# FFN output with h stationary, weights and v by casting DMA, filler matmuls: a sketch attention and ReGLU FFN on one core

## Chip, cores, metric

One core of a Trainium2 chip. The metric is the device time of one execution in microseconds (us), as the median of several. A measurement of this kernel tells about 1% from no change.

## What is computed

Polynomial-sketch attention, then a ReGLU FFN on its output:

```python
# q, k, v: (4, 4, 1088, 32); S1, S2: (8, 32); w_gate, w_val: (128, 1536); w_out: (1536, 128)
def phi(x):                                   # (..., 32) -> (..., 64)
    a = einsum('rd,bhsd->bhsr', S1, x); b = einsum('rd,bhsd->bhsr', S2, x)
    return einsum('bhsi,bhsj->bhsij', a, b).reshape(*x.shape[:-1], 64)
q_p, k_p = phi(q), phi(k)
kv  = einsum('bhsf,bhsd->bhfd', k_p, v)
z   = sum(k_p, axis=2)
num = einsum('bhsf,bhfd->bhsd', q_p, kv)
den = einsum('bhsf,bhf->bhs', q_p, z)[..., None] + 1e-6
x   = (num / den).transpose(0, 2, 1, 3).reshape(4352, 128)
out = (maximum(x @ w_gate, 0) * (x @ w_val)) @ w_out
```

## The kernel before

The 4352 tokens are cut into eight FFN chunks of 512 (two of each batch) and a ninth of 256 with the rest of all batches (`REST`). An FFN chunk has 12 slots, one for each 128 of d_ff; 108 slots in all, which the code counts as `n`. In a slot PE multiplies xT by a 128x128 piece of w_gate (`ffn_g`, L540) and of w_val (`ffn_v`, L551), ScalarE takes the relu of the first (`ffn_relu`, L545), VectorE multiplies (`ffn_mul`, L556, into ht), and three slots later (`LAG`) PE adds w_out's part to `ot_ps` (`ffn_out`, L384), with w_out stationary and 512 tokens moving, so that the output comes out feature-major. At a chunk's end ScalarE evicts ot to fp16 (`ffn_fin0`, L390), PE transposes it back in pieces of 128 tokens (`ffn_fin1`, L398), ScalarE evicts that to `o_sb` (`ffn_fin2`, L404), and SyncE's queue stores it.

Each batch needs its attention before its two chunks. For k: two VectorE transposes into kT (L175), 16 small fp32 matmuls with S (`k_ab_mm`, L187), two transposes back (kab, L194), products on VectorE or GpSimd (`k_outer`, kp, L210), nine pairs of matmuls with v into kv_ps (`k_kv`, L228), z (`k_z`, L247), its copy zs (`k_zs`), one more matmul (`k_sz`, L257), w_s (`k_sw`), and kvb (`k_fin`). For q: the same transposes, matmuls with S and with w_s (L187, L299), denominator, products (qp, L210), PE transposes (`q_xpose`, L348), eviction on ScalarE (`q_ev`, qpt, L354), the numerator (`q_num`, L369) and xT on ScalarE (`q_x`, L373).

PSUM: two banks each for g and v, one for ot, one for kv, and a ring of two (`ps_a`) for all else: the S matmuls, z, q's transposes, the numerator, and the output's transposes.

Loads: S1 and S2 on ScalarE's queue; k and q on SyncE's; v on GpSimd's, cast to fp16 on the way, in four pieces a batch (`load_v`, L93). Batch 0's v is issued near the start. w_gate and w_val are loaded as fp32 once the second kT transpose of batch 0 is done, w_out behind k of batch 1, and ScalarE casts each to fp16 (`cast_w`, L422). k and q of batch b+1 are issued behind the second q transpose of batch b.

The order on every engine is written out by a planner: each step has a key (its place), an engine, a cost, what it needs and which PSUM buffers it takes and frees. `run` goes through time and gives each engine the first step by key that can start, with landing times from `LAND`; steps of batches 1 to 3 start at T0 = 19 us of its clock at the earliest. The engines then run that order, each strictly in turn, and wait for one another by semaphores.

Of the kernel before, what the change touches and what calls it, by code (L numbers as in the profile page):

```python
# [16 lines left out]
KLEAD, QLEAD, VLEAD, LAG = 40, 20, 44, 3  # L17
WAIT, T0 = 0.02, 19.0
LAND = {"s": 4.8, "k": (5.0, 12.0, 15.0, 20.0), "q": (7.0, 13.0, 16.0, 21.0), "v": 8.0, "w": (11.0, 13.0, 15.0)}
# [3 lines left out]
def kernel(  # L23
# [66 lines left out]
    def load_v(b, g):  # L90
        x = v[b].rearrange("h (t c) d -> t h (c d)", t=32)
        n = NC + 1 if g < 2 else NC
        nc.gpsimd.dma_start(  # L93
            out=v4[b][32 * g:32 * g + 32, :, 0:n].rearrange("p h c d -> p h (c d)"),
            in_=x[:, :, CB[g] * D:(CB[g] + n) * D],
        )
# [7 lines left out]

    w_in = [big.tile([128, NJ, 128], FP32, name=f"w_in{i}") for i in range(3)]
# [13 lines left out]
    for g in range(4):  # L119
        load_v(0, g)  # L120
# [14 lines left out]
    nc.scalar.activation(out=warm, in_=warm, func=ACTF.Relu)  # L135

# [40 lines left out]
    def k_transpose(b, i):  # L177
        transpose_in(kT[b % 2], k4[b], i)

# [3 lines left out]
    def ab_mm(key, xt, n, c0, lo=0):  # L183

        for rp in range(2):
            for g in range(4):
# [35 lines left out]
    def k_kv(b, c):  # L222
        if c == 0:
            st["kv", b] = ps_k.tile([128, 2, 64], FP32, name="kv_ps")
        ps = st["kv", b]
        np = SL if c == NC else 128
        for p in range(2):
            i = nc.tensor.matmul(ps[:, p].rearrange("p (h d) -> p h d", h=2),  # L228
                                 st["kp", b, c][0:np, p * 128:(p + 1) * 128],
                                 v4[b][0:np, 2 * p:2 * p + 2, c],  # L230
                                 start=(c == 0 and p == 0), stop=(c == NC), skip_group_check=True)
            if c == 0 and p == 0:
                first = i
            elif c == 0 and not MANUAL:
                tc.add_manual_dep(
                    i.ins, first.ins.name,
                    mybir.DependencyInfo(mybir.DependencyClass.NoSync, mybir.DependencyReason.DATA),
                    reason="the first one clears the bank's written bits")
# [17 lines left out]
    def k_sz(b):  # L256
        nc.tensor.matmul(st["z", b][:, HR:2 * HR], s1f4.rearrange("p h d -> p (h d)"), st["zs", b],  # L257
                         start=True, stop=True, skip_group_check=True)
# [75 lines left out]
    def q_outer(key, c0, c1, eng):  # L334
        np, m = q_np(key), c1 - c0
        qp = php.tile([128, m, H * F], FP16, name=f"qp{m}")
        outer(eng, qp[0:np].rearrange("p c (h i j) -> p (c h) i j", h=H, i=R),
              st["a2", key][0:np, c0 * H:c1 * H], q_ab(key, 1, c0, c1), np, m * H)
        for c in range(c0, c1):
            st["qp", key, c] = qp[:, c - c0]  # L340


    def q_xpose(key, p0, c):
# [3 lines left out]
        for p in range(2):  # L347
            nc.tensor.transpose(st["qpt", key, p0][:, p, c * n:(c + 1) * n],  # L348
                                st["qp", key, p0 + c][0:n, p * 128:(p + 1) * 128], ident16[0:n, 0:n])

    def q_ev(key, p0):
        n = q_np(key)
        t = php.tile([128, 2, 512], FP16, name="qpt")
        nc.scalar.copy(out=t[:, :, 0:4 * n], in_=st["qpt", key, p0][:, :, 0:4 * n])  # L354
        st["qpts", key, p0] = t

    def q_num(key, p0):
# [4 lines left out]
        if key == REST:  # L362
            for b in range(B):
                for p in range(2):
                    nc.tensor.matmul(ps[64 * p:64 * p + 64, b * n:(b + 1) * n], kvb[b][:, p],
                                     t[:, p, b * n:(b + 1) * n], start=True, stop=True)
            return
        for p in range(2):
            nc.tensor.matmul(ps[64 * p:64 * p + 64], kvb[key[0]][:, p], t[:, p], start=True, stop=True)  # L369
# [9 lines left out]
    def ffn_out(n):  # L379
        i, j = divmod(n, NJ)  # L380
        cs = CH[i][1]
        if j == 0:
            st["ot", i] = ps_o.tile([128, 512], FP32, name="ot_ps")
        nc.tensor.matmul(st["ot", i][:, :cs], wo_sb[:, j], st["ht", i][:, j, :cs],  # L384
                         start=(j == 0), stop=(j == NJ - 1))

    def ffn_fin0(i):
        cs = CH[i][1]
        ot = fo.tile([128, 512], FP16, name="ot16")
        nc.scalar.copy(out=ot[:, :cs], in_=st["ot", i][:, :cs])  # L390
        st["ot16", i] = ot

    def ffn_fin1(i):
        cs = CH[i][1]
        ps = ps_a.tile([128, 4, DM], FP16, name="ps_a")
        st["ott", i] = ps
        for t in range(cs // 128):
            nc.tensor.transpose(ps[:, t], st["ot16", i][:, t * 128:(t + 1) * 128], ident16)  # L398

    def ffn_fin2(i):  # L400
        cs = CH[i][1]
        n = cs // 128
        o = fo.tile([128, 4, DM], FP32, name="o_sb")
        nc.scalar.mul(out=o[:, :n], in_=st["ott", i][:, :n], mul=1.0 / (XSCALE * XSCALE))  # L404
        if n == 4:
# [15 lines left out]
    def cast_w(i):  # L421
        nc.scalar.copy(out=(wg_sb, wv_sb, wo_sb)[i], in_=w_in[i])  # L422

# [6 lines left out]
    RING = {"g": 2, "v": 2, "o": 1, "k": 1, "a": 2}  # L430
    LAT = {"PE": 0.24, "ACT": 0.16, "DVE": 0.15, "POOL": 0.2, "SP": 0.0}
# [4 lines left out]
    def run():  # L436
# [5 lines left out]
        while any(todo.values()):  # L442
            best = None
            for e, q in todo.items():
                pick = None
                for s in q:
                    if any(n not in made for n in s[6]):
                        continue
                    t = max([clock[e], s[10]] + [made[n] for n in s[6]])
# [18 lines left out]
            todo[s[2]].remove(s)  # L468
            for r in s[8]:
# [10 lines left out]
    def plan_k(b, s, pieces, d=1.0, t0=0.0):  # L480
# [11 lines left out]
        at(s + 6 * d, "PE", 0.45, k_z, b, need=[("kab", b)], make=("z", b), take="a")  # L492
        at(s + 8 * d, "DVE", 0.12, k_zs, b, need=[("z", b)], make=("zs", b))
        at(s + 9 * d, "PE", 0.15, k_sz, b, need=[("zs", b)], make=("sz", b))
        at(s + 11 * d, "DVE", 0.13, k_sw, b, need=[("sz", b)], make=("w", b), free="a")
        for c in range(NC + 1):
            at(s + (8 + 0.8 * c) * d, "PE", 0.075, k_kv, b, c,
               need=[("kp", b, of[c]), ("v4", b), ("kv", b, c - 1) if c else ("kab", b)], make=("kv", b, c),
               take="k" if c == 0 else "")
        at(s + 16 * d, "DVE", 0.22, k_fin, b, need=[("kv", b, NC)], make=("kvb", b), free="k")  # L500
# [62 lines left out]
    made["s"], made["v4", 0] = LAND["s"], LAND["v"]  # L563
    for i in range(3):
        made["win", i] = LAND["w"][i]

    def plan_v(b, s, t0):
        for g in range(4):
            at(s + 0.1 * g, "POOL", 0.65, load_v, b, g, make=("v4i", b, g), t0=t0)
        at(s + 0.5, "SP", 0.01, lambda: None, need=[("v4i", b, g) for g in range(4)], make=("v4i", b))  # L570
        at(s + 0.5, "SP", 2.5, lambda: None, need=[("v4i", b)], make=("v4", b))


    for i in range(3):
        at(-39 + i, "ACT", 1.4, cast_w, i, need=[("win", i)], make=("w", i))
# [15 lines left out]
    for n in range(NSLOT):  # L591
# [58 lines left out]
```

## Time and profile before

| what | value |
|---|---|
| median of 3 runs | 136.62 us (136.24 to 137.31) |
| the profiled execution | 137.69 us, its span 135.6 us |
| busy: PE, VectorE, ScalarE, GpSimd | 104.1, 95.6, 84.6, 50.7 us |
| instructions on PE: matmuls, weight loads | 838, 838 |
| granted clock over the span | 0.969 |

PE is TensorE's matmuls, PEld its loads of the stationary operand, DVE VectorE, ACT ScalarE, POOL GpSimd, SP SyncE; a q behind the name is the engine's queue of DMA issues and control instructions. A matmul's duration in the trace includes its way through the array, so that matmuls in a row overlap: how fast they follow one another is seen in the chain that ended last, where each stands with the time until the next. The granted clock is shown as 1.00 until a change is recorded.

### The profile page before, as it was taken

How to read it: one execution, taken by the hardware profiler on the slowest of the kernel's cores; microseconds unless marked ns; L12 is line 12 of the kernel's file. 1: busy time of each engine (PE TensorE's matmuls, PEld its weight loads, DVE VectorE, ACT ScalarE, POOL GpSimd, SP SyncE). 2: the span in 40 equal slices, each digit the busy share in tenths (PEclk: the TensorE clock that was granted, in tenths of full speed). 3: DMA queues.
4: the chain of work that ended last, by engine and by line, in shares of the span. 5: the costliest groups of instructions: out<-in, count | busy, mean ns of one | idle time of the engine just before them, and what ended most of it. 6: DMA issues, size and time to landing. Idle time of an engine off the chain costs nothing.

```text
span 135.6 us, 2420 instructions
## 1 busy us (share of the span) xinstructions
PE 104.1 (77%) x838; PEld 48.4 (36%) x838; DVE 95.6 (70%) x198; ACT 84.6 (62%) x149; POOL 50.7 (37%) x72
## 2 busy tenths in 40 slices
PE   0007774599999875999779999999999999999100
PEld 0002432224443442334245445445443444465000
DVE  2046888228999774999968769999758999998000
ACT  3000442677266775857838955997999999986200
POOL 7401725937859991001599203946000000000000
PEclk9999999999999999999999999999999999999755
DMA  4935996292635019100011010011011011010110
GB/s 127 220 73 145 357 302 224 28 99 78 252 47 60 0 21 333 43 35 0 6 37 41 6 46 30 2 30 48 0 34 46 7 39 36 25 49 15 47 40 18
DMA packets 7059, 10.33 MB, mean 76 GB/s; under 512 B 776, under 2 KB 4616, under 8 KB 7048
## 3 DMA queue, kind: packets, MB, share of 16 engines
q1 hardware_dynamic: 4324, 8.98, 20.0%
q0 software_dynamic: 2304, 1.12, 7.2%
q10 hardware_dynamic: 420, 0.10, 0.3%
q8 instruction: 6, 0.10, 0.3%
q14 instruction: 5, 0.04, 0.1%
HBM read 9.08 MB, written 2.23 MB: 83 GB/s over the span
## 4 chain that ended last, share of the span: by engine, by line
PE 58%; DMA 14%; DVE 11%; ACT 8%; issue 2%; ACTq 1%; SPq 0%; DVEq 0%
PE v_ps L551 15%; PE g_ps L540 15%; PE ot_ps L384 14%; DVE ht L556 6%; DMA w_in<-in_moe_w_out_dram 6%; DMA xall<-in_S_dram 5%; PE ps_a L187 5%; ACT g_sb L545 4%; DMA k<-in_k_dram 3%; PE ps_a L369 2%; PE ps_a L348 2%; DVE qT L175 1%; PE kv_ps L228 1%; PE ps_a L299 1%; PE ps_a L398 1%
## 5 line engine op out<-in xcount | busy, mean ns | idle before, releaser
L556 DVE TENSOR_TENSOR ht<-g_sb,v_ps 128x512 f16<-128x512 f16 (+1 forms) x108 | 66.5, 649 | 10.2 <-PE v_ps L551 3.3
L545 ACT ACTIVATE g_sb<-g_ps 128x512 f16<-128x512 f32 (+1 forms) x108 | 60.1, 583 | 21.2 <-PE g_ps L540 8.8
L551 PE MATMUL v_ps<-xT,wv_sb 128*128 128x512 f16 (+1 forms) x108 | 40.4, 374 | 1.6 <-DVE ht L556 1.4
L540 PE MATMUL g_ps<-xT,wg_sb 128*128 128x512 f16 (+1 forms) x108 | 39.1, 378 | 2.8 <-ACT g_sb L545 2.3
L384 PE MATMUL ot_ps<-ht,wo_sb 128*128 128x512 f16 (+1 forms) x108 | 39.6, 368 | 0.4
L210 POOL TENSOR_TENSOR kp<-kab 128x512 f16<-128x512 f32 (+2 forms) x16 | 17.0, 1086 | 11.0 <-DVE kab L194 11.0
L210 POOL TENSOR_TENSOR qp<-a,qab 128x512 f16<-128x512 f32 (+2 forms) x18 | 17.6, 1000 | 4.8 <-DVE a L330 3.5
L551 PEld LDWEIGHTS <-wv_sb 128*128 128x128 f16 x108 | 10.6, 98 | 12.8 <-issue 6.7
L384 PEld LDWEIGHTS <-wo_sb 128*128 128x128 f16 x108 | 10.6, 98 | 9.7 <-issue 3.3
L540 PEld LDWEIGHTS <-wg_sb 128*128 128x128 f16 x108 | 10.5, 101 | 10.0 <-issue 2.3
L187 PE MATMUL ps_a<-kT,s_bd 64*32 64x288 f32 x64 | 4.7, 549 | 10.1 <-DVE kT L175 10.1
L348 PE MATMUL ps_a<-ident,qp 128*128 128x128 f16 (+1 forms) x72 | 9.9, 236 | 2.7 <-POOL qp L210 1.5
L315 POOL TENSOR_TENSOR bw<-qab,qw 128x256 f32<-128x256 f32 (+2 forms) x5 | 3.3, 655 | 21.1 <-DVE qw L306 21.1
L348 PEld LDWEIGHTS <-qp 128*128 128x128 f16 (+1 forms) x72 | 6.0, 103 | 10.5 <-POOL qp L210 2.8
L228 PEld LDWEIGHTS <-kp 128*128 128x128 f16 (+1 forms) x72 | 6.0, 105 | 9.6 <-issue 4.2
L93 POOL DMA_DIRECT2D v<-in_v_dram x16 | 9.0, 568 | 0.1
L354 ACT COPY qpt<-ps_a 128x1024 f16<-128x1024 f16 (+1 forms) x9 | 9.0, 999 | 0.0
L228 PE MATMUL kv_ps<-v,kp 128*128 128x64 f16 (+1 forms) x72 | 8.0, 205 | 0.9 <-DVE kp L210 0.9
L422 ACT CAST wg_sb<-w_in 128x1536 f16<-128x1536 f32 x1 | 1.5, 1472 | 11.5 <-DMA w_in<-in_moe_w_gate_dram 11.5
L175 DVE STREAM_TRANSPOSE kT<-k 128x544 f32<-128x544 f32 x8 | 5.5, 718 | 2.8 <-DMA k<-in_k_dram 2.8
L175 DVE STREAM_TRANSPOSE qT<-q 128x544 f32<-128x544 f32 x8 | 5.8, 724 | 2.3 <-DMA q<-in_q_dram 2.3
L373 ACT CAST xT<-ps_a 128x512 f16<-128x512 f32 (+1 forms) x9 | 5.3, 588 | 1.1 <-PE ps_a L369 0.7
(60 smaller groups left out, 71.9 us busy)
## 6 DMA issues: line engine op xcount, KB each, us to landing
q<-in_q_dram SPq DMA_DIRECT2D x4, 544.0 KB
out_dram<-o_sb SPq DMA_DIRECT2D x16, 128.0 KB
k<-in_k_dram SPq DMA_DIRECT2D x3, 544.0 KB
w_in<-in_moe_w_gate_dram SPq DMA_DIRECT2D x1, 768.0 KB
w_in<-in_moe_w_val_dram SPq DMA_DIRECT2D x1, 768.0 KB
w_in<-in_moe_w_out_dram SPq DMA_DIRECT2D x1, 768.0 KB
v<-in_v_dram POOLq DMA_DIRECT2D x8, 72.0 KB, 2.8
k<-in_k_dram SPq DMA_DIRECT2D x2, 272.0 KB
```

Source lines behind the costliest of these rows:

```text
L93: nc.gpsimd.dma_start(out=v4[b][32 * g:32 * g + 32, :, 0:n].rearrange("p h c d -> p h (c d)"), in_=x[:, :, CB[g] * D:(CB[g] + n) * D],)
L175: st["last"] = nc.vector.transpose(out=dst[:, a:e], in_=src[:, a:e])
L187: nc.tensor.matmul(st["ps", key][rp][32 * g:32 * g + 32, lo:lo + 32 * n], s_bd[64 * rp:64 * rp + 64].rearrange("p h r x -> p (h r x)"), xt ...
L210: eng.tensor_tensor(out=dst, in0=a[:, :, :, None].to_broadcast([np, n, R, R]), in1=bb[:, :, None, :].to_broadcast([np, n, R, R]), op=ALU.mult)
L228: i = nc.tensor.matmul(ps[:, p].rearrange("p (h d) -> p h d", h=2), st["kp", b, c][0:np, p * 128:(p + 1) * 128], v4[b][0:np, 2 * p:2 * p + ...
L348: nc.tensor.transpose(st["qpt", key, p0][:, p, c * n:(c + 1) * n], st["qp", key, p0 + c][0:n, p * 128:(p + 1) * 128], ident16[0:n, 0:n])
L354: nc.scalar.copy(out=t[:, :, 0:4 * n], in_=st["qpt", key, p0][:, :, 0:4 * n])
L384: nc.tensor.matmul(st["ot", i][:, :cs], wo_sb[:, j], st["ht", i][:, j, :cs], start=(j == 0), stop=(j == NJ - 1))
L540: nc.tensor.matmul(st["g", n][:, :cs], wg_sb[:, j], xT[:, c0:c0 + cs], start=True, stop=True)
L545: nc.scalar.activation(out=st["gs", n][:, :cs], in_=st["g", n][:, :cs], func=ACTF.Relu)
L551: nc.tensor.matmul(st["v", n][:, :cs], wv_sb[:, j], xT[:, c0:c0 + cs], start=True, stop=True)
L556: nc.vector.tensor_tensor(out=st["ht", i][:, j, :cs], in0=st["gs", n][:, :cs], in1=st["v", n][:, :cs], op=ALU.mult)
```

## The change

- `ffn_out`: h is the stationary operand, in pieces of 128 tokens, and w_out's piece (128 columns) moves; so ot is token-major. The eviction to fp16, the transposes and the second eviction fall away; one eviction (`ffn_fin`) with the scaling writes `o_sb`, and the stores are a step of their own.
- Weights: loaded by GpSimd's queue straight into the fp16 tiles (a cast on the way), behind batch 0's v; no fp32 copies and no casts on ScalarE.
- Batch 0's v is issued behind the first kT transpose of batch 0. S2 goes to GpSimd's queue, ahead of everything else there; S1 stays.
- z lives in kv's bank: `k_z` takes that bank, and its first matmuls clear it; kv and the w_s matmul start without clearing. A bank of the ring of two is not taken any more.
- Filler matmuls (128x128 zeros by 128 columns) fill PE's planned gaps from 2.5 us of the planner's clock until the first g; they use ot's bank.
- The S matmuls go through their column groups in the outer loop; q's products lie in one tile of four; the planner knows the four g_sb buffers.

```diff
-LAND = {"s": 4.8, "k": (5.0, 12.0, 15.0, 20.0), "q": (7.0, 13.0, 16.0, 21.0), "v": 8.0, "w": (11.0, 13.0, 15.0)}
+LAND = {"s": 3.5, "k": (5.2, 12.0, 15.0, 20.0), "q": (6.8, 13.0, 16.0, 21.0)}
+NFILL = 200
...
     def load_v(b, g):
...
+        behind(st["kt0"] if b == 0 else None, i)
...
-    for i, sm in enumerate((S1, S2)):
-        nc.scalar.dma_start(out=xall[:, i], in_=sm[None].to_broadcast([16, R, D]))
+    for sm, i, eng in ((S1, 0, nc.scalar), (S2, 1, nc.gpsimd)):
+        eng.dma_start(out=xall[:, i], in_=sm[None].to_broadcast([16, R, D]))
...
-    def load_w(i, after):
+    def load_w(i):
...
-        behind(after, nc.sync.dma_start(out=w_in[i], in_=x))
+        nc.gpsimd.dma_start(out=(wg_sb, wv_sb, wo_sb)[i], in_=x)
...
+    zeros = const.tile([128, 128], FP16, name="zeros")
+    nc.vector.memset(zeros, 0.0)
...
     def ab_mm(key, xt, n, c0, lo=0):
-        for rp in range(2):
-            for g in range(4):
+        for g in range(4):
+            for rp in range(2):
...
     def k_kv(b, c):
-        if c == 0:
-            st["kv", b] = ps_k.tile([128, 2, 64], FP32, name="kv_ps")
...
-                                 start=(c == 0 and p == 0), stop=(c == NC), skip_group_check=True)
+                                 start=False, stop=(c == NC), skip_group_check=True)
...
     def k_z(b):
-        ps = ps_a.tile([128, 512], FP32, name="ps_a")
-        st["z", b] = ps
+        bank = ps_k.tile([128, 192], FP32, name="kv_ps")
+        st["kv", b] = bank[:, 0:128].rearrange("p (a d) -> p a d", a=2)
+        st["z", b] = ps = bank[:, 128:192]
...
     def ffn_out(n):
         i, j = divmod(n, NJ)
-        cs = CH[i][1]
         if j == 0:
-            st["ot", i] = ps_o.tile([128, 512], FP32, name="ot_ps")
-        nc.tensor.matmul(st["ot", i][:, :cs], wo_sb[:, j], st["ht", i][:, j, :cs],
-                         start=(j == 0), stop=(j == NJ - 1))
-
-    def ffn_fin0(i):
...
-    def ffn_fin1(i):
...
-    def ffn_fin2(i):
...
+            st["ot", i] = ps_o.tile([128, 4, DM], FP32, name="ot_ps")
+        for t in range(CH[i][1] // 128):
+            nc.tensor.matmul(st["ot", i][:, t], st["ht", i][:, j, t * 128:(t + 1) * 128], wo_sb[:, j],
+                             start=(j == 0 and t == 0), stop=(j == NJ - 1), skip_group_check=True)
+
+    def ffn_fin(i):
+        n = CH[i][1] // 128
         o = fo.tile([128, 4, DM], FP32, name="o_sb")
-        nc.scalar.mul(out=o[:, :n], in_=st["ott", i][:, :n], mul=1.0 / (XSCALE * XSCALE))
+        nc.scalar.mul(out=o[:, :n], in_=st["ot", i][:, :n], mul=1.0 / (XSCALE * XSCALE))
+        st["o", i] = o
+
+    def ffn_store(i):
...
-    def cast_w(i):
-        nc.scalar.copy(out=(wg_sb, wv_sb, wo_sb)[i], in_=w_in[i])
...
+            if ("g", 0) in made:
+                todo["PE"] = [s for s in todo["PE"] if s[4] is not fill]
...
+    plan_v(0, -50, 0, need=[("kT", 0, 0)])
     for i in range(3):
...
-        at(-39 + i, "ACT", 1.4, cast_w, i, need=[("win", i)], make=("w", i))
+        at(-49 + i, "POOL", (0.8, 0.6, 1.1)[i], load_w, i, make=("wi", i), t0=0.0, need=[("v4i", 0, 3)])
+        at(-49 + i, "NONE", 5.0, None, need=[("wi", i)], make=("w", i))
...
+    def fill():
+        if "fill" not in st:
+            st["fill"] = ps_o.tile([128, 4, DM], FP32, name="ot_ps")
+        nc.tensor.matmul(st["fill"][:, 0], zeros, zeros, start=True, stop=True)
+
+    for n in range(NFILL):
+        at(1000 + n, "PE", 0.1, fill, t0=2.5)
```

## Rows read from the trace of the kernel before

**Rows 1.** Windows: length, busy us (instructions) by engine, clock, DMA share, GB/s.

```profile
9.00:18.00 9.00, 5.91 (x82) 2.89 (x83) 6.84 (x17) 2.42 (x2) 3.27 (x4) 1.00 0.66 221
...
26.60:52.00 25.40, 23.81 (x208) 10.70 (x208) 18.44 (x38) 16.50 (x29) 19.45 (x23) 1.00 0.46 94
52.00:106.00 54.00, 50.46 (x409) 22.93 (x405) 45.21 (x86) 42.45 (x76) 18.58 (x20) 1.00 0.12 39
106.00:119.00 13.00, 13.00 (x64) 5.96 (x63) 12.61 (x20) 12.49 (x23) 0.00 (x0) 1.00 0.09 28
```

**Rows 2.** The page's chain that ended last: shares of the span by engine.

```profile
PE 58%; DMA 14%; DVE 11%; ACT 8%; issue 2%; ACTq 1%; SPq 0%; DVEq 0%
```

**Rows 3.** The same chain in order of time, 0 to 36 us: start, us, what.

```profile
1.57 7.09 DMA xall<-in_S_dram
...
10.14 1.84 PE ps_a L187 x16
...
15.26 7.58 DMA w_in<-in_moe_w_out_dram
...
22.86 1.47 ACT wo_sb L422
24.34 0.92 ACT qpt L354
...
25.30 0.65 PE ps_a L369 x2
...
26.61 0.59 PE g_ps L540
...
28.26 0.43 PE v_ps L551
...
32.56 0.34 PE ps_a L369 x2
...
33.46 0.22 PE v_ps L551
```

**Rows 4.** Timeline, 0 to 30 us: start, us, engine, instruction [idle before, releaser].

```profile
1.52 2.34 POOL L93 DMA_DIRECT2D v<-in_v_dram  x4
...
9.35 1.37 DVE L175 STREAM_TRANSPOSE kT<-k 128x544 f32<-128x544 f32 x2
...
10.74 0.33 SPq L110 DMA_DIRECT2D w_in<-in_moe_w_gate_dram  x1
...
17.05 1.47 ACT L422 CAST wv_sb<-w_in 128x1536 f16<-128x1536 f32 x1 [0.38 <-DMA w_in<-in_moe_w_val_dram]
...
20.62 1.33 PE L348 MATMUL ps_a<-ident,qp 128*128 128x128 f16 x8 [1.21 <-DVE qp L210]
```

**Rows 5.** Timeline, 66 to 68 us: batch 3's 16 k matmuls.

```profile
66.58 0.72 PE L187 MATMUL ps_a<-kT,s_bd 64*32 64x288 f32 x16
```

**Rows 6.** The chain that ended last, 72 to 114 us.

```profile
72.77 0.48 ACT ot L390
...
113.91 0.22 PE ps_a L398 x4
```

**Rows 7.** Timeline, 50 to 54 us: the numerator of batch 1, kT of batch 3.

```profile
50.89 0.41 PE L369 MATMUL ps_a<-qpt,kvb 128*64 128x512 f16 x2 [0.74 <-ACT o_sb L404]
...
52.84 0.74 DVE L175 STREAM_TRANSPOSE kT<-k 128x544 f32<-128x544 f32 x1 [2.52 <-DMA k<-in_k_dram]
```

**Rows 8.** Who waited for whom: us in total, times, longest us.

```profile
DVE zs L253 <- PE ps_a L247: 1.3, 2, 1.1
```

**Rows 9.** Timeline, 124 to 127 us: the end of the work.

```profile
124.64 1.01 PE L384 MATMUL ot_ps<-ht,wo_sb 128*128 128x256 f16 x3
...
125.69 0.37 ACT L390 CAST ot<-ot_ps 128x256 f16<-128x256 f32 x1 [0.93 <-PE ot_ps L384]
...
126.44 0.38 ACT L404 ACTIVATE o_sb<-ps_a 128x256 f32<-128x256 f16 x1 [0.38 <-PE ps_a L398]
```

**Rows 10.** Groups by line: busy us, mean ns of one; idle before.

```profile
L384 PEld LDWEIGHTS <-wo_sb 128*128 128x128 f16 x108 | 10.6, 98 | 9.7 <-issue 3.3
```

More of the change, by code (lines that the diff above doesn't have):

```diff
@@ L178, in k_transpose @@
         transpose_in(kT[b % 2], k4[b], i)
+        st.setdefault("kt0", st["last"])
     def q_transpose(b, i):
@@ L227, in k_kv @@
         for p in range(2):
-            i = nc.tensor.matmul(ps[:, p].rearrange("p (h d) -> p h d", h=2),
+            nc.tensor.matmul(ps[:, p].rearrange("p (h d) -> p h d", h=2),
                                  st["kp", b, c][0:np, p * 128:(p + 1) * 128],
                                  v4[b][0:np, 2 * p:2 * p + 2, c],
-                                 start=(c == 0 and p == 0), stop=(c == NC), skip_group_check=True)
[L232 to L238, printed above, removed]
+                                 start=False, stop=(c == NC), skip_group_check=True)
     def k_z(b):
-        ps = ps_a.tile([128, 512], FP32, name="ps_a")
-        st["z", b] = ps
+        bank = ps_k.tile([128, 192], FP32, name="kv_ps")
+        st["kv", b] = bank[:, 0:128].rearrange("p (a d) -> p a d", a=2)
+        st["z", b] = ps = bank[:, 128:192]
         ab = st["ab", ("k", b)]
@@ L257, in k_sz @@
         nc.tensor.matmul(st["z", b][:, HR:2 * HR], s1f4.rearrange("p h d -> p (h d)"), st["zs", b],
-                         start=True, stop=True, skip_group_check=True)
+                         start=False, stop=True, skip_group_check=True)
     def k_sw(b):
@@ L334, in q_outer @@
     def q_outer(key, c0, c1, eng):
[L335 to L340, printed above, removed]
+        np, p0 = q_np(key), c0 // 4 * 4
+        if ("qp", key, p0) not in st:
+            st["qp", key, p0] = php.tile([128, 4, H * F], FP16, name="qp")
+        outer(eng, st["qp", key, p0][0:np, c0 - p0:c1 - p0].rearrange("p c (h i j) -> p (c h) i j", h=H, i=R),
+              st["a2", key][0:np, c0 * H:c1 * H], q_ab(key, 1, c0, c1), np, (c1 - c0) * H)
     def q_xpose(key, p0, c):
@@ L348, in q_xpose @@
             nc.tensor.transpose(st["qpt", key, p0][:, p, c * n:(c + 1) * n],
-                                st["qp", key, p0 + c][0:n, p * 128:(p + 1) * 128], ident16[0:n, 0:n])
+                                st["qp", key, p0][0:n, c, p * 128:(p + 1) * 128], ident16[0:n, 0:n])
     def q_ev(key, p0):
         n = q_np(key)
-        t = php.tile([128, 2, 512], FP16, name="qpt")
+        t = php.tile([128, 2, 512], FP16, name="qptx")
         nc.scalar.copy(out=t[:, :, 0:4 * n], in_=st["qpt", key, p0][:, :, 0:4 * n])
-        st["qpts", key, p0] = t
+        st["qpts", key, p0] = [t[:, p, 0:4 * n].rearrange("p (c t) -> p c t", c=4) for p in range(2)]
     def q_num(key, p0):
@@ L365, in q_num @@
                     nc.tensor.matmul(ps[64 * p:64 * p + 64, b * n:(b + 1) * n], kvb[b][:, p],
-                                     t[:, p, b * n:(b + 1) * n], start=True, stop=True)
+                                     t[p][:, b], start=True, stop=True)
             return
         for p in range(2):
-            nc.tensor.matmul(ps[64 * p:64 * p + 64], kvb[key[0]][:, p], t[:, p], start=True, stop=True)
+            nc.tensor.matmul(ps[64 * p:64 * p + 64].rearrange("p (c t) -> p c t", c=4), kvb[key[0]][:, p], t[p],
+                             start=True, stop=True)
     def q_x(key, p0):
@@ L380, in ffn_out @@
         i, j = divmod(n, NJ)
-        cs = CH[i][1]
         if j == 0:
-            st["ot", i] = ps_o.tile([128, 512], FP32, name="ot_ps")
-        nc.tensor.matmul(st["ot", i][:, :cs], wo_sb[:, j], st["ht", i][:, j, :cs],
-                         start=(j == 0), stop=(j == NJ - 1))
-    def ffn_fin0(i):
[L388 to L391, printed above, removed]
-    def ffn_fin1(i):
[L394 to L398, printed above, removed]
-    def ffn_fin2(i):
-        cs = CH[i][1]
-        n = cs // 128
-        o = fo.tile([128, 4, DM], FP32, name="o_sb")
-        nc.scalar.mul(out=o[:, :n], in_=st["ott", i][:, :n], mul=1.0 / (XSCALE * XSCALE))
-        if n == 4:
+            st["ot", i] = ps_o.tile([128, 4, DM], FP32, name="ot_ps")
[4 more added lines that the diff above has]
+        n = CH[i][1] // 128
+        o = fo.tile([128, 4, DM], FP32, name="o_sb")
+        nc.scalar.mul(out=o[:, :n], in_=st["ot", i][:, :n], mul=1.0 / (XSCALE * XSCALE))
+        st["o", i] = o
+    def ffn_store(i):
+        o = st["o", i]
+        if CH[i][1] == 512:
             b, hf = divmod(i, 2)
@@ L448, in run @@
                         continue
-                    t = max([clock[e], s[10]] + [made[n] for n in s[6]])
+                    t = max([0.0 if e == "NONE" else clock[e], s[10]] + [made[n] for n in s[6]])
                     ok = True
@@ L468, in run @@
             todo[s[2]].remove(s)
+            if s[2] == "NONE":
+                made[s[7]] = t + s[3]
+                continue
             for r in s[8]:
@@ L562, with plan_v @@
     made["k4", 0, 0] -= 0.8
-    made["s"], made["v4", 0] = LAND["s"], LAND["v"]
-    for i in range(3):
[L565 to L574, printed above, removed]
-        at(-39 + i, "ACT", 1.4, cast_w, i, need=[("win", i)], make=("w", i))
+    made["s"] = LAND["s"]
+    def plan_v(b, s, t0, need=()):
+        for g in range(4):
+            at(s + 0.1 * g, "POOL", 0.55, load_v, b, g, need=need, make=("v4i", b, g), t0=t0)
+        at(s + 0.5, "NONE", 2.5, None, need=[("v4i", b, g) for g in range(4)], make=("v4", b))
+    plan_v(0, -50, 0, need=[("kT", 0, 0)])
+    for i in range(3):
+        at(-49 + i, "POOL", (0.8, 0.6, 1.1)[i], load_w, i, make=("wi", i), t0=0.0, need=[("v4i", 0, 3)])
+        at(-49 + i, "NONE", 5.0, None, need=[("wi", i)], make=("w", i))
     plan_k(0, -38, ((0, 1, "POOL"), (1, 3, "DVE"), (3, 4, "POOL"), (4, 6, "DVE"), (6, 7, "POOL"), (7, 8, "DVE"),
```

36 lines of the change are left out of this document (14 added, 22 removed).

## The prediction

> **What bounds the kernel now.** I read the windows first, then the chain that ended last, then the timeline where the chain leaves TensorE. The windows [rows 1] give two stages. Up to 26.6 us no FFN matmul runs and no engine is full: it is a chain of latencies. From 26.6 us on three engines are close together: in 106 to 119 us PE is busy 13.00 of 13.00, VectorE 12.61, ScalarE 12.49; in 52 to 106 us they reach 50.46, 45.21 and 42.45 of 54. So in the FFN stage there is little to win on any one engine, and the head is where time lies loose. Over the whole span the chain is 58% PE [rows 2]: 78.6 us, of which some 5 lie in the head, so about three quarters of the 99.0 us from the first FFN matmul at 26.61 [rows 3] to the end of the last output matmuls, 124.64 + 1.01 [rows 9].
>
> The head's chain [rows 3] is: S lands at 1.57 + 7.09 = 8.66; transposes; 16 k matmuls of 1.84; and then a surprise, the load of w_out, 15.26 to 22.84, its cast on ScalarE (22.86, 1.47), and only then the eviction of the transposed q products (24.34), the numerator (25.30), xT and the first g at 26.61. The timeline [rows 4] shows why: the eight q transposes had ended at 20.62 + 1.33 = 21.95, but the eviction stands behind the cast in ScalarE's queue.
>
> The third thing is TensorE's clock. The column of the granted clock reads 1.00 in every window here [rows 1], yet the chain steps from one 512-column matmul to the next in 0.43 us around 28 us and in 0.22 us at 33.46 [rows 3]: 512 columns at 1.2 and at 2.4 GHz. I go by the steps: PE runs at the lower level until about 31.6, after several us of dense matmuls.
>
> **Part by part, the head.** S2 moves from ScalarE's queue to GpSimd's, and v's four loads, which were issued at 1.52 over 2.34 us [rows 4], move behind the first kT transpose. Before S lands the queues carry, by the shapes, k and q of batch 0 (1.11 MB), v (0.28 as written) and S (0.03). Without v 0.20 of the bytes go; v is read as fp32 and written as fp16, so counted by what is read it is 0.33. Of 7.09 us that is 1.4 to 2.4; I take 1.9. The bounds are 0 (a small transfer that waits for k's and q's packets as before) and 3.2 (S before k and q are through).
>
> The 16 k matmuls end 11.98, 1.26 after the second kT transpose (9.35 + 1.37 = 10.72) [rows 3, 4]. The same 16 at the upper level take 0.72 in all [rows 5]. If the filler matmuls (about 110 by my count of the planned gaps, each 128 columns of zeros) hold the clock up, that is worth 0.6. The two numerator matmuls go from 0.65 to 0.34 on the chain [rows 3]: 0.3. The q matmuls and transposes gain too, 0 to 1, which I leave to the range. A filler stands in PE's queue ahead of real work; the plan puts 0.1 each only into gaps, and late real work waits for the fillers of one gap at most, a us at the lower level. I take 0, because real landings have been later than planned gaps.
>
> The casts go: ScalarE is free at 21.95 instead of 24.34, 2.3 us on the chain after the 0.1 it needs to start. What is late next? The weights themselves. They now come through GpSimd's queue, after v: first kT transpose done at about 8.2 (10.05 less 1.9), four v issues of 0.585 [rows 4] to 10.5, then gate, val, out. In the kernel before, gate and val took from 10.74 to 17.05 [rows 4], 6.3 us; from 10.5 that is 16.8, and if all of k and q of batch 1 (1.11 MB at the 221 GB/s of 9 to 18 us [rows 1], 5.0 us) get ahead of them, 21.8. The chain brings x at 26.61 - 1.9 - 0.6 - 0.3 - 2.3 = 21.5, so the weights are about in time. GpSimd's own k products wait behind the seven issues, to about 8.2 + 7 x 0.585 = 12.3, some 2 us after the k matmuls' results (11.98 - 2.5 = 9.5, and their transposes); what hangs on them alone is k's state, wanted by the numerator at 25.30 - 4.8 = 20.5. I cost that at nothing under this cover; without it up to 2. Head: -5.0 (bounds -7.5 and -2.3).
>
> **First slots.** From 26.61 to 31.65 seven FFN steps on the chain run at 0.43 [rows 3]; at 0.22 they would save 1.5. ScalarE with 0.6 a slot takes over, so I take -1.3; 0 if the clock is low, -2 with the k matmuls of batch 1.
>
> **The FFN.** A slot's output was one matmul of 512 columns with the weights stationary; now it is four of 128 with h stationary, 300 more pairs of load and matmul. The trace has this shape: the output transposes, four with 128x128 fp16 stationary and 128 columns each, take 0.22 on the chain [rows 6], no more than one 512-column matmul [rows 3]. So 55 ns a pair, loads hidden: +0 to +0.5 over 102 full slots, I take +0.3. The transposes themselves go: up to 8 x 0.22 = 1.8 off PE in this stage. The first eviction stays where it was (the chain waits 0.48 for the ot bank to be emptied [rows 6]; one buffer before and after), but the second one and its PSUM bank go. The numerator's wait of 0.74 for o_sb to release that bank [rows 7] goes: 0.7. VectorE's wait of 2.52 for k of batch 3 [rows 7] stays: that load is still issued behind batch 2's q transposes.
>
> Added is a wait. z and kv now share one PSUM tile; if reads by VectorE and writes by PE in it are kept in order, kv matmuls queue behind zs and w_s on VectorE, with FFN matmuls behind them on PE; and zs behind kv matmuls that wait for GpSimd's products. No row shows it. The nearest is zs waiting for z, 1.3 us in two cases [rows 8]: 0 to 1.3 for each of three batches; z also leaves the two-bank ring, which could gain as much. I take 0.3 each, 0.9, nearer to 0 since zs follows z at once in most cases. The Trainium skill, "PSUM — Partial Sum Buffer", section "PSUM bank collisions raise a hardware error", says engines must be kept apart by whole bank and quadrant, not by address, which speaks against this sharing. By that rule the 0.9 is due; without it the sum would be 0.9 lower; no row here decides.
>
> FFN: +0.3 - 1.8 - 0.7 + 0.9 = -1.3 (bounds +3 and -3.5).
>
> **Tail.** After the last ot matmul come an eviction (125.69), two transposes and a second eviction (126.44) [rows 9]. Only one eviction stays: -0.75. The stores behind it are the same.
>
> **Sum.** -5.0 - 1.3 - 1.3 - 0.75 = -8.35. The profiled execution took 137.69, 1.07 above the median, so 129.3 there and 128.3 as a median.
>
> **Rivals.** (B) *The head's gain is given back.* Chunk 2 needs batch 1's attention; if k and q of batch 1 land behind 2.36 MB of weights, the FFN starts early and then waits for x as late as before. For it: the numerator at 50.89 [rows 7] is just ahead of chunk 2's first matmul. Against: the matmuls of batch 1's k stood behind slow PE work until 29, and that goes. All but 1.5 of the 6.3 lost: 133.1.
>
> (C) *The pairs are dearer in a long stream.* Four transposes between 512-column matmuls [rows 6] do not prove 100 us of them. Half hidden, midway between 55 and the 98 ns of the load row [rows 10], a pair is 76.5: 102 x 4 x 21.5 ns = 8.8 on PE, three quarters of it on the chain, 6.6: 134.9, a gain about as small as can be told. The Trainium skill, "TensorE: Matmul & The Clock Gate", section "Back-to-back issue gap", gives about 81 ns for 128 columns in a sustained stream of load and matmul pairs; by that, as an estimate, the time would be 136.3, no change. The trace's 55 in a group of four differs; a stream of them no row shows.
>
> (D) *Loads are not hidden at all.* If the 98 ns of the load row [rows 10] is the step where loads follow one another with only 128 columns beside them: 102 x 4 x 43 ns = 17.5, three quarters of it 13.2: 141.5, slower. It makes the kernel slower than before from a pair of about 82 ns on (8.35 / 0.75 / 408 = 27 ns over 55). Against it: loads of 98 ns already overlap in those transposes.
>
> (E) *The fillers do not do what they say.* PE idles between them, or falls back before the FFN: 0.6 + 0.3 + 1.3 lost, 130.5.
>
> **How the numbers follow.** Forecast 57%, B 17%, E 15%, C 6%, D 5% with other late waits. The forecast's own bounds are wider than plausible together (122.9 to 136.6); 124 to 134 holds most of it and B and E, and leaves C, D and the extremes out. A change of 1% is about what can be told from none: below 135.3 lie the forecast, B and E, 0.89; C, which straddles that bound, I count as no change, 0.06; D is 0.05.
>
> **What would show it.** The first g_ps matmul at 20.5 to 22.5 with steps of 0.22 at once; S at about 6.8; no cast on ScalarE; the output's pairs at 55 ns in the chain; one eviction at the end. It is wrong if the first g is early but the first g of chunk 2 is not (B), if the output's steps are above 60 ns (C, D), or if kv and zs stand in the waits with more than a us (bank).

## The result, and the profile after

The changed kernel takes 131.8 us (median of four; 131.28 to 134.17) where the kernel before, beside it, took 136.97 (136.24 to 137.59): a ratio of 0.959 [0.952, 0.967] (a fifth run, of 130.56, counts in it), faster, by 5.2 to 5.6 us. The forecast was 128.3, a gain of 8.35, so the time lies inside the range, 3.5 us above the forecast, and the gain falls short by some 3. Runs more than 1.5% above the fastest of the same kernel are left out of the ratios, the profiled executions of the changed kernel (134.17, span 132.1) and of the output part with its order kept (experiment 2) among them, so these two traces are read for what waits for what, and sizes are taken from the ratios.

**The head came as forecast.** The chain of the changed kernel, 1 to 23 us (start, us, what), to be laid beside [rows 3]:

```profile
1.34 3.87 DMA xall<-in_S_dram
...
6.62 1.71 PE ps_a L190 x16
8.33 2.04 PE ot_ps L595 x18
10.37 0.63 PE kv_ps L243 x18
...
20.43 0.34 PE ps_a L364 x2
...
21.44 0.38 PE g_ps L527
...
22.05 0.22 PE v_ps L538
22.27 0.23 PE g_ps L527
```

S lands at 5.21 instead of 8.66, no cast and no load of weights is left on the chain, and the first g comes at 21.44 instead of 26.61. The steps behind it are 0.22, not 0.43. What is new on the chain is 18 filler matmuls (L595), 2.04 us of them, between the k matmuls and z (the 18 kv_ps matmuls of L243).

**Then a load comes late.** Who waits for whom (us in total, times, longest):

```profile
DVE kT L177 <- DMA k<-in_k_dram: 9.3, 2, 6.7
```

In the kernel before the longest of these waits was the 2.52 of [rows 7], and there the load of k of batch 3 was issued ahead of the store of chunk 0:

```profile
49.17 0.33 SPq L78 DMA_DIRECT2D k<-in_k_dram  x1
...
50.86 1.23 SPq L413 DMA_DIRECT2D out_dram<-o_sb  x2
```

The queue of SyncE in the changed kernel, 20 to 60 us, and VectorE's transposes that wait for these loads:

```profile
23.85 0.33 SPq L81 DMA_DIRECT2D k<-in_k_dram  x1
24.23 0.43 SPq L81 DMA_DIRECT2D q<-in_q_dram  x1
41.29 1.23 SPq L399 DMA_DIRECT2D out_dram<-o_sb  x2
43.77 0.34 SPq L81 DMA_DIRECT2D k<-in_k_dram  x1
44.16 1.15 SPq L81 DMA_DIRECT2D q<-in_q_dram  x1
...
30.66 0.74 DVE L177 STREAM_TRANSPOSE kT<-k 128x544 f32<-128x544 f32 x1 [2.64 <-DMA k<-in_k_dram]
...
51.61 1.37 DVE L177 STREAM_TRANSPOSE kT<-k 128x544 f32<-128x544 f32 x2 [6.69 <-DMA k<-in_k_dram]
...
53.61 0.58 PE L538 MATMUL v_ps<-xT,wv_sb 128*128 128x512 f16 x1 [5.57 <-DVE ht L543]
```

The store of chunk 0 (41.29) stands ahead of the load of k of batch 3 (43.77). That load lands at 51.6, and behind VectorE's wait for it PE idles 5.57. The chain has the load with "43.77 7.81 DMA k". (The wait of 2.64 for batch 2's k belongs to this one execution: three experiments below whose queue is the same up to there waited 0.36, 0.90 and not at all. The wait for batch 3's k does not: the kernel without fillers of experiment 6, with the same queue, waited 6.95.) The windows show what the engines and the clock did (length, busy us by engine PE, PEld, DVE, ACT, POOL, granted clock, share of the 16 DMA engines, GB/s):

```profile
43.80:47.00 3.20, 3.20 (x42) 1.90 (x46) 1.12 (x2) 3.05 (x6) 2.31 (x2) 1.00 0.73 208
47.00:49.50 2.50, 1.04 (x24) 0.25 (x9) 0.00 (x0) 0.79 (x2) 0.00 (x0) 1.00 0.65 219
49.50:51.60 2.10, 0.00 (x0) 0.00 (x0) 0.00 (x0) 0.00 (x0) 0.00 (x0) 1.00 0.13 55
...
52.00:58.00 6.00, 4.39 (x25) 2.40 (x25) 5.40 (x10) 1.19 (x2) 0.00 (x0) 0.50 0.01 2
...
66.00:104.00 38.00, 37.88 (x416) 23.36 (x415) 32.33 (x60) 31.51 (x58) 14.48 (x16) 1.00 0.08 25
```

In the last 2.1 us before k is there no engine works at all and the DMA engines are busy by 0.13, which is 2.1 of 16, as if what is left hung on two engines; experiment 3 tests that. Then the granted clock is 0.50 for 6 us, with PE idle before it: the 1.2 GHz level, at which the steps take 0.43 again.

**The output stage and the end.** From 66 to 104 us PE is busy 37.88 of 38.00. The groups (busy us, mean ns of one), then the chain at the end, then two of the longest waits around z and kv:

```profile
L380 PE MATMUL ot_ps<-wo_sb,ht 128*128 128x128 f16 x408 | 41.2, 222 | 0.2
L380 PEld LDWEIGHTS <-ht 128*128 128x128 f16 x408 | 31.5, 99 | 20.2 <-issue 4.8
```

```profile
114.48 0.22 PE ot_ps L380 x4
...
121.01 0.11 PE ot_ps L380 x2
...
121.34 0.11 PE ot_ps L380 x2
...
123.91 0.30 PE ot_ps L380 x2
124.21 0.02 issue
124.23 0.38 ACT o_sb L386
```

```profile
PEld ps_a L295 <- DVE w_s L257: 0.8, 1, 0.8
...
POOL kp L213 <- PE kv_ps L229: 0.4, 1, 0.4
```

Four pairs of load and matmul move the chain by 0.22, two by 0.11: 55 ns a pair, to the end of the output stage, though a load alone takes 99 and a matmul from start to end 222. Of the 63 groups of four on the chain between 66 and 118 us 59 take 0.22. Neither of the last two rows is a wait for the shared bank itself: the first is q's matmuls waiting for w_s, the second GpSimd waiting for kv matmuls ahead of its next product. VectorE's one wait for that bank, w_s behind kv matmuls, is 0.2. One eviction (124.23) is left where [rows 9] had two and the transposes between them.

### The profile page after: what moved, and what is told of

Its sections match the earlier page's. It is cut to its first block, busy times and chain, and to the rows that moved or that the text cites. A ratio compares the mean times of both kernels' runs of the same rounds, so it can differ in the third digit from the quotient of the medians.

```text
span 132.1 us, 3190 instructions
## 1 busy us (share of the span) xinstructions
PE 110.1 (83%) x1225; PEld 68.0 (51%) x1225; DVE 97.3 (74%) x199; ACT 75.2 (57%) x137; POOL 53.0 (40%) x76
## 4 chain that ended last, share of the span: by engine, by line
PE 60%; DMA 14%; DVE 14%; issue 3%; ACT 2%; POOL 1%; DVEq 0%; POOLq 0%
PE v_ps L538 17%; PE ot_ps L380 16%; PE g_ps L527 15%; DMA k<-in_k_dram 11%; DVE ht L543 5%; PE ps_a L190 3%; DMA xall<-in_S_dram 3%; PE ps_a L343 3%; PE ot_ps L595 2%; ACT g_sb L532 2%; DVE kp L213 2%; DVE kT L177 1%; PE ps_a L364 1%; DVE qp L213 1%; PE kv_ps L229 1%
## 5 line engine op out<-in xcount | busy, mean ns | idle before, releaser
L532 ACT ACTIVATE g_sb<-g_ps 128x512 f16<-128x512 f32 (+1 forms) x108 | 58.8, 580 | 28.4 <-PE g_ps L527 26.2
L380 PEld LDWEIGHTS <-ht 128*128 128x128 f16 x408 | 31.5, 99 | 20.2 <-issue 4.8
L380 PE MATMUL ot_ps<-wo_sb,ht 128*128 128x128 f16 x408 | 41.2, 222 | 0.2
L527 PE MATMUL g_ps<-xT,wg_sb 128*128 128x512 f16 (+1 forms) x108 | 37.7, 374 | 1.0 <-ACT g_sb L532 0.7
L349 ACT COPY qptx<-ps_a 128x1024 f16<-128x1024 f16 (+1 forms) x9 | 8.8, 974 | 15.5 <-PE ps_a L343 15.3
L538 PEld LDWEIGHTS <-wv_sb 128*128 128x128 f16 x108 | 10.8, 100 | 6.0 <-issue 4.6
L595 PE MATMUL ot_ps<-zeros 128*128 128x128 f16 x121 | 11.3, 255 | 1.1 <-DVE zeros L137 1.1
L595 PEld LDWEIGHTS <-zeros 128*128 128x128 f16 x121 | 9.5, 118 | 2.2 <-DVE zeros L137 1.1
L527 PEld LDWEIGHTS <-wg_sb 128*128 128x128 f16 x108 | 9.8, 99 | 0.7
L343 PEld LDWEIGHTS <-qp 128*128 128x128 f16 (+1 forms) x72 | 5.5, 97 | 5.5 <-POOL qp L213 2.0
L386 ACT ACTIVATE o_sb<-ot_ps 128x512 f32<-128x512 f32 (+1 forms) x9 | 5.2, 574 | 2.6 <-PE ot_ps L380 2.4
```

The source lines that it names most:

```text
L380: nc.tensor.matmul(st["ot", i][:, t], st["ht", i][:, j, t * 128:(t + 1) * 128], wo_sb[:, j], start=(j == 0 and t == 0), stop=(j == NJ - 1) ...
L527: nc.tensor.matmul(st["g", n][:, :cs], wg_sb[:, j], xT[:, c0:c0 + cs], start=True, stop=True)
L532: nc.scalar.activation(out=st["gs", n][:, :cs], in_=st["g", n][:, :cs], func=ACTF.Relu)
L538: nc.tensor.matmul(st["v", n][:, :cs], wv_sb[:, j], xT[:, c0:c0 + cs], start=True, stop=True)
L595: nc.tensor.matmul(st["fill"][:, 0], zeros, zeros, start=True, stop=True)
```

## The experiments

All are compared with the kernel before on the same chip; a ratio has its 95% interval.

**1. Only the order of two entries in SyncE's queue.** In the changed kernel the store of chunk 0 is put behind the loads of batch 3, where it stood before the change:

```
 for _, s in order:
+    if s[4] == ffn_store and s[5] == (0,):
+        continue
     s[4](*s[5])
     if s[4] == q_transpose and ...:
         load_kq(k4, k, s[5][0] + 1, st["last"])
         load_kq(q4, q, s[5][0] + 1)
+        if s[5][0] + 1 == 3:
+            ffn_store(0)
```

> The changed kernel (131.8 us), and only the store of chunk 0 put behind the loads of k and q of batch 3 in SyncE's queue. Theory K: the wait for k of batch 3 (6.7 us) falls to 2 to 3, the one for k of batch 2 (2.6 us) stays, the clock stays up: 127 to 129.5 us, which is the forecast's 128.3, made with a wait of 2.52 for k of batch 3 left in. Rival (k of batch 3 is late because it is issued late, whatever stands ahead of it): 130.5 to 132 us, the wait 5 us or more.

127.3 us (126.75 to 127.86), 0.926 [0.922, 0.930]. The queue, the transpose, the waits and the window behind them:

```profile
41.85 0.33 SPq L81 DMA_DIRECT2D k<-in_k_dram  x1
42.22 0.80 SPq L81 DMA_DIRECT2D q<-in_q_dram  x1
43.12 1.23 SPq L399 DMA_DIRECT2D out_dram<-o_sb  x2
...
45.52 1.37 DVE L177 STREAM_TRANSPOSE kT<-k 128x544 f32<-128x544 f32 x2 [2.52 <-DMA k<-in_k_dram]
```

```profile
DVE kT L177 <- DMA k<-in_k_dram: 2.9, 2, 2.5
```

```profile
46.00:56.00 10.00, 7.83 (x78) 4.07 (x75) 9.93 (x21) 5.28 (x10) 1.57 (x3) 1.00 0.12 40
```

k lands in 45.52 - 41.85 = 3.7 us instead of 7.8, the wait is 2.52 as in the kernel before, and the granted clock stays at 1.00. The ratio falls by 0.033, which is 4.5 us of 137 (3.3 to 5.7 with the two intervals), for the order of a store and a load: the whole shortfall of 3 and more. The rival is out.

**2. Which part of the change moved the store.** The kernel before with the token-major output alone (ffn_out, one ffn_fin, and the store as a step of the plan), everything else as it was:

```
-at(... "ACT" ..., ffn_fin0, ...); at(... "PE" ..., ffn_fin1, ...); at(... "ACT" ..., ffn_fin2, ...)
+at(n + LAG, "ACT", 0.29 if f < 1 else 0.48, ffn_fin, i, need=[("o", n)], make=("f2", i), free="o")
+at(n + LAG + 4, "SP", 1.0, ffn_store, i, need=[("f2", i)], make=("f3", i))
```

> The kernel before with one part of the change: the output written token-major by pairs of weight load and matmul, one eviction, no transposes, the store a step of its own in the plan. Weights, z, v and S1 and S2 as before, no fillers. In this kernel the store of chunk 0 stands ahead of the load of k of batch 3 in SyncE's queue, where it stood behind it before. By the forecast's terms for the output (pairs +0.3, transposes -1.8, bank wait -0.7, end -0.75) and nothing else: -2.95, 134.0 to 134.6 us. Theory K (the store ahead of the load delays k of batch 3): VectorE waits 4 us or more for k of batch 3, where it waited 2.5, the step right behind runs at the lower clock, and the gain is gone: 135.5 to 139 us, no first steps moved. Rival: the pairs themselves are slower than the matmul they replace in parts of the stream; then the chain shows output steps of more than 0.25 us away from any wait for k.

141.8 us (140.69 to 143.23), 1.031 [1.015, 1.047]: this part alone makes the kernel slower, and by 2.8 more than the expectation's upper end; what makes it so much stays open. Queue, transpose, waits and windows:

```profile
46.71 1.24 SPq L403 DMA_DIRECT2D out_dram<-o_sb  x2
48.82 0.34 SPq L78 DMA_DIRECT2D k<-in_k_dram  x1
...
57.90 0.74 DVE L175 STREAM_TRANSPOSE kT<-k 128x544 f32<-128x544 f32 x1 [7.88 <-DMA k<-in_k_dram]
```

```profile
52.00:55.00 3.00, 0.00 (x0) 0.00 (x0) 0.00 (x0) 0.00 (x0) 0.00 (x0) 1.00 0.57 178
55.00:57.90 2.90, 0.00 (x0) 0.00 (x0) 0.01 (x1) 0.00 (x0) 0.00 (x0) 0.79 0.12 41
```

The picture is the same with the old head: with one eviction less and the store a step of its own, the store of chunk 0 is emitted before q of batch 2 is transposed, and so ahead of k of batch 3. The same kernel with the edit of the first experiment:

> The kernel before with only the token-major output (141.8 us, slower than before by 3%), and the store of chunk 0 put behind the loads of k and q of batch 3 in SyncE's queue, where it stood in the kernel before. Nothing else differs. Theory K (the order of these two in the queue is what cost): VectorE's wait for k of batch 3 falls from 7.9 us to 2.5 to 3.5, the dip of the granted clock behind it goes, and the time is 134 to 136.5 us, about the forecast's -2.95 for the output alone. Rival (the token-major output itself, or another order that the plan made with it, costs): 138 to 141 us with k in time.

135.0 us (132.82 to 137.09), with k issued at 47.84 and a wait of 2.94. The ratio, 0.970 [0.965, 0.975], rests on the two fastest of the four runs; the medians alone, 135.0 and 137.5, would give 0.982. So the output alone is worth 4.1 us (0.030 x 137.5) with the order kept, or 2.5 by the medians, and costs 4.2 (0.031 x 137.9) with the order that the plan gave it. One thing expected did not come in the profiled execution: the granted clock still fell behind the wait, to 0.50 from 55 to 58 us. Of 67 output steps on its chain behind 60 us 61 take 0.22, so the rival's slow pairs are not there either.

**3. The loads earlier, the store over more engines.** Two edits that are not part of the change. The first issues k and q of batches 2 and 3 behind the second k transpose of the batch ahead, not its second q transpose:

```
-if s[4] == q_transpose and s[5][1] == 1 and ...:
+if s[4] == (k_transpose if s[5] and s[5][0] else q_transpose) and s[5][1] == 1 and ...:
```

> The changed kernel (131.8 us) with k and q of batches 2 and 3 issued behind the second kT transpose of the batch ahead, not behind its second qT transpose; all engine orders but the queue of SyncE stay. Theory K: the FFN stage lost what the head gained because VectorE, strictly in order, waits for k (9.3 us in two waits after, 2.8 before); then both waits all but vanish and the time falls by 5 to 7 us, to 125 to 127, and the first g of chunk 4 comes as much earlier. Rival P: the stage is slower because of PE (pairs of load and matmul, z and kv in one bank); then the waits go but the time stays at 130.5 to 132.

125.1 us (124.36 to 126.7), 0.906 [0.902, 0.910]; the loads now go out at 20.35 and 30.78, far ahead of the store at 39.99, and no wait of VectorE for k is left. The second leaves the loads where the change has them and writes a chunk as four transfers whose slowest dimension has 32 rows, instead of two whose slowest dimension has 2 (shortened):

```
-for g0 in (0, 2):   d = [[w * DM, 2], d.ap[0], [1, 4 * DM]]   from o[32*g0 : 32*g0 + 64]
+for g in range(4):  d = [d.ap[0], [1, 4 * DM]]                 from o[32*g : 32*g + 32]
```

> The changed kernel with each chunk's output stored by four transfers of 32 rows in place of two of 2 x 32 rows, loads where they were. Theory S, a part of K: a store with a slowest dimension of 2 runs on two of the 16 DMA engines, some 20 packets a us, and k of batch 3, issued behind chunk 0's store, waits on those two; then stores run at over 100 packets a us, the wait for k of batch 3 falls from 6.7 to 3 or 4, and the end after the last eviction shortens by up to 1.5: 127.5 to 129.5. The wait for batch 2 (2.6) stays, no store is near it. Rival: the load is slow by itself (its issue, or v beside it): no change but the end, 130.5 to 132.

126.44 us (125.67 to 126.94), 0.918 [0.914, 0.922]. The wait remains but is shorter:

```profile
DVE kT L177 <- DMA k<-in_k_dram: 4.4, 2, 3.5
```

The same store still stands ahead of the load, but it no longer sits on two engines: the load lands in 4.6 us (42.15 to 46.78). So the order costs what it does because of the store's shape. Not all of the gain is this wait, which is why the time lies below what was expected: batch 2's k was waited for only 0.90, and the end is shorter. From the end of the last eviction to the end of the span it is 6.2 us here, 7.5 in the changed kernel, so the two-engine stores hold up the end as well.

A chunk's store alone shows it, as the share of 16 engines, in two windows of the first experiment's kernel (two transfers of 64 rows) and one of the kernel with both edits (four of 32):

```profile
115.00:116.00 1.00, 0.91 (x10) 0.49 (x8) 0.95 (x4) 0.45 (x2) 0.00 (x0) 1.00 0.13 47
116.00:117.00 1.00, 0.55 (x4) 0.20 (x4) 0.30 (x1) 0.32 (x1) 0.00 (x0) 1.00 0.12 43
```

```profile
110.00:111.00 1.00, 1.00 (x13) 0.82 (x11) 0.96 (x3) 0.97 (x3) 0.00 (x0) 1.00 0.58 150
```

0.13 of 16 is 2.1 engines. The Trainium skill, "DMA: Bandwidth & Descriptors", section "Why a DMA increments its semaphore by 16 and not by 1", says that a transfer uses the largest number of engines up to 16 that divides the slowest dimension of both its sides; by that the old store has two engines and the new one 16. The trace agrees on the first (0.13); on the second it shows that 0.58 of 16 is at least nine. Both edits together:

> Both edits. Theory K with S: the early load already removes the wait, so the stores add only the shorter end: 124 to 126, at most 1.5 under the early load alone. Rival P: 130 to 132.

123.28 us (122.98 to 123.77), 0.896 [0.893, 0.899], better than either and a little below what was expected.

**4. The same two edits in the kernel before.**

> The kernel before with two edits that have nothing to do with the change: the loads of k and q of batches 2 and 3 are issued behind the second k transpose of the batch ahead instead of its second q transpose, and the store of each chunk is four transfers of 32 rows instead of two of 64. Theory K (what the change gives was there in full and the late loads of k took part of it back): VectorE's two waits for k (2.8 us in 2 before) are gone here as well, the end is shorter by about 1.4 as with the 16-way store on the changed kernel, so 131 to 133.5 us; against the 123.3 of the changed kernel with the same two edits the change is then worth 8 to 10 us, about the terms of the forecast. Rival P (the parts of the change are themselves worth only 5 to 6 us and the loads are a separate gain that the kernel before could not have used): 128 to 130 us, so that the difference to 123.3 stays at 5 to 6. Rival N (the kernel before is bound elsewhere, its waits for k were hidden): only the end moves, 135.5 to 136.5 us.

132.9 us (132.41 to 133.37), 0.968 [0.957, 0.980]. The kernel before gains 0.032, the changed one 0.959 - 0.896 = 0.063. With k in time in both, the change is worth 0.968 - 0.896 = 0.072 of 137.5, 9.9 us (with the two intervals, 8.3 to 11.5). The rival that had the change itself at 5 to 6 us is out. Part of the earlier kernel's gain is again the end: 8.8 us from the last eviction to the end of the span before, 6.4 here, 6.3 in the changed kernel with both edits.

**5. The shared bank of z and kv.** The kernel of both edits, with z back in a ps_a bank of its own (`ps_a.tile(...)` in k_z, start=True again for s·z and the first kv matmul, the planner's rings as before):

> The changed kernel with the two load edits (123.3 us), and z back in a ps_a bank of its own as in the kernel before, so kv of a batch no longer waits for the bank that holds z, but z takes one of the two ps_a banks again. If the shared bank costs what the forecast took (0.9): 122.2 to 122.6 us. If the bank wait is as small as the waits of the changed kernel's trace (0.2 to 0.8 each, off the chain): 123.0 to 123.6, no difference. If the ps_a ring is what the change freed: 123.8 to 125, with waits for ps_a banks longer than 1 us ahead of the q matmuls or transposes.

122.29 us (121.89 to 123.52), 0.894 [0.879, 0.909]: no answer at this width. Again, the kernel of both edits and this one side by side:

> The changed kernel with both load edits, again, as the partner of the next run on the same chip: 122.5 to 124 us.

> The same with z in a bank of its own, 122.3 against 123.3 us so far on different chips. If the shared bank costs the forecast's 0.9: 0.6 to 1.2 us below the run beside it. If it costs nothing that a measurement tells: within 0.5 us of it.

122.53 (121.78 to 123.09), 0.893 [0.890, 0.896], and 121.91 (120.88 to 122.91), 0.886 [0.882, 0.890]. The difference is 0.007, 0.9 us, with an interval of 0.2 to 1.6. The size is the forecast's 0.9, its mechanism does not show: in the trace of the kernel of both edits the waits that name the bank are short,

```profile
PEld kv_ps L253 <- DVE zs L249: 0.3, 1, 0.3
...
DVE w_s L257 <- PE kv_ps L229: 0.2, 1, 0.2
```

and the plan changes its order on VectorE and PE with the bank. Which of the two makes the difference stays open. This is the fastest kernel of the study.

**6. The fillers.** The changed kernel without any of them (`fill()` does nothing, every other order the same):

> The changed kernel without the filler matmuls, all other orders as they are. If the fillers hold the clock at 2.4 GHz (the prediction): the 16 k matmuls are as slow as with them at first, but the numerator takes 0.65, the first FFN steps 0.43 for some us, the first g comes 0.5 to 1 later, in all 1.5 to 2.5 us more: 133.3 to 134.3. Rival: the FFN's wait for k eats that too (chunk 2 and kT of batch 2 come no earlier): 131.5 to 132.5.

134.06 us (132.95 to 134.95), 0.972 [0.967, 0.976], where the change has 0.959: the fillers are worth 1.2% (0.3 to 2.1). The first g comes at 22.52, and the matmuls of 512 columns behind it last 0.59 to 0.63 each, against 0.38 with the fillers:

```profile
22.52 0.59 PE L527 MATMUL g_ps<-xT,wg_sb 128*128 128x512 f16 x1 [0.35 <-ACT xT L369]
```

And the kernel of both edits with only the 35 fillers ahead of the first k matmuls:

```
 for _, s in order:
+    if s[4] is fill and ("ps", ("k", 0)) in st:
+        continue
```

> The changed kernel with the two load edits (123.3 us), and only the 35 filler matmuls that stand ahead of the first k matmuls; the 86 behind them are left out (18 of these stand between the k matmuls and z and lie on the chain for 2.04 us of the changed kernel). Theory clock (the later ones hold the granted clock at its higher level until the first g): without them it falls back and is at the higher level only from the first FFN steps on, the first g comes 0.5 to 1.5 us later, 124 to 126 us. Rival path (the 18 fillers cost more as work ahead of z than their clock gives): z starts up to 1 us earlier, the first g at 20.5 to 21.2, 122.3 to 123.0 us.

123.97 us (123.3 to 125.1), 0.904 [0.891, 0.917], against 123.28 with all: not told apart by the time. The window of 9 to 21 us says why, first with 35 fillers, then with all 121:

```profile
9.00:21.00 12.00, 8.01 (x100) 4.09 (x101) 10.95 (x27) 1.25 (x2) 8.40 (x14) 0.50 1.13 212
```

```profile
9.00:21.00 12.00, 9.63 (x180) 7.30 (x179) 11.26 (x28) 1.45 (x2) 8.23 (x13) 1.00 1.11 210
```

The time lies between the two that were expected, and both are half right. Without the later fillers PE, busy 8.0 of 12 us, is granted 0.50, and the first g takes 0.59 where it takes 0.38 with all; but z no longer stands behind 18 fillers, and the first g starts at 21.40, only 0.20 later than with all.

## Why the prediction was right in range and 3.5 us too low

- **The step that failed** is one term of the FFN sum: "VectorE's wait of 2.52 for k of batch 3 stays". The wait became 6.7 us and took the clock with it. The sentence gave the condition of the load's issue rightly (behind batch 2's q transposes, unchanged) but not what stands ahead of it: taking one eviction and the transposes out of the output, and making the store a planned step, moved the store of chunk 0 past the load in SyncE's queue. The prediction looked at the queue that the weights and v are moved past, GpSimd's, and not at the order of stores and loads in SyncE's; "the stores behind it are the same" speaks of the end only. Price: 4.5 us in the whole change (experiment 1), 8.4 in the output part alone (experiment 2, 1.031 against 0.970; 6.7 by the medians).
- **With that one order put back** the kernel takes 127.3 beside its own 137.5, a gain of 10.2 where 8.35 was forecast with 2.52 for k left standing. So the rest of the sum was low by 1.8. Some of that is the term "the stores behind it are the same", put at nothing: the end behind the last eviction took 8.8 us before (126.82 to 135.6) and 7.7 in experiment 1 (117.06 to 124.8). The rest is not traced to a term.
- **Head**, forecast -5.0: the first g at 21.44 against 21.5. That it fits so closely is luck, since three terms were off and cancel. S landed at 5.21, not 6.8. The k matmuls gained 0.1, not 0.6 (1.71 instead of 1.84, ending 1.14 behind the transpose instead of 1.26): PE had idled 2.02 us ahead of them, and the granted clock reads 0.51 from 7.4 to 10.8 us. And z, whose input was there at 9.21, began at 10.30, since 18 fillers stand ahead of it. The forecast had these fillers at 0; z pays 1.1 us for them, though by experiment 6 the first g comes no sooner when they are left out (21.40 against 21.20). No run takes the parts of the head singly; their sizes are read off the chain.
- **First slots**, -1.3: steps of 0.22 at once, as forecast. Of E the first part came, the 0.6 of the k matmuls, and the rest did not; without fillers it does (22.52, matmuls of 0.59 to 0.63).
- **Pairs**, +0.3: 55 ns a pair to the end of the output stage, so C and D are out. The Trainium skill's figure of 81 ns for a sustained stream of pairs ("TensorE: Matmul & The Clock Gate", "Back-to-back issue gap") is not what this trace shows: 59 of 63 groups of four take 0.22. The groups stand between matmuls of 512 columns; an unbroken stream of pairs no run shows.
- **Transposes, second eviction, its bank, and the end**: forecast -1.8, -0.7, -0.75 and with the pairs -2.95; measured by the output part with its order kept, 4.1, or 2.5 by the medians (experiment 2). At the end alone, from the last output matmul to the end of the last eviction, 1.17 us became 0.40 (124.21 to 124.61): 0.77, as forecast.
- **Bank**, +0.9: undoing it gave 0.9 (0.2 to 1.6), of unsettled cause, so the match may be luck.
- **B** foresaw that the head's gain would be given back by a late load of k, and most of it was; but not by batch 1's k behind the weights. It was batch 3's k behind a store.

## What to carry to other kernels

When an edit shortens or removes a step, list again, queue by queue, the order in which the DMAs are issued, the stores too: a store that becomes ready sooner can slip ahead of a load that everything waits for. Give each store a slowest dimension that spreads over all DMA engines, since a load behind a store on two engines ends only when these two get to it. And issue a load when its buffer is free, not when some later step of the batch ahead comes by: that alone was worth 7.3 us here (0.959 to 0.906), more than the 5.2 to 5.6 of the change as it was.

## What the runs showed of the hardware

- A load of 544 KB that landed in 3.7 to 4.1 us took 7.8 to 9.1 with a chunk's store (two transfers of 128 KB, each on two engines) ahead of it in its queue; for the last 2 to 3 us only 0.12 to 0.13 of the DMA engines were busy. With that store on four transfers of 32 rows it took 4.6.
- Behind the last eviction the same two-engine stores took 7.5 to 8.8 us to the end of the span, and 6.2 to 6.4 with 32 rows each, in the kernel before as in the changed one.
- The granted clock fell to 0.50 after PE had idled 5.57 us (6 us at that level), and to 0.50 in the profiled execution of the output part with its order kept (55 to 58 us), where PE had idled 2.87 in one piece. In experiment 1, where PE idled 1.40, it stayed at 1.00.
- Ahead of the first recorded change the clock's column reads 1.00 whatever the level: without fillers it reads 1.00 from 9 to 21 us and the next g and v matmuls last 0.59 to 0.63; with 35 fillers ahead it reads 0.50 and they last the same. The matmuls are the safer reading, as in the kernel before.
